# Attention and two feed-forward layers on one core: weight conversions start late in attention, and a first phase of four units

## The chip, the cores and the metric

The kernel runs on one core of one Trainium2 chip. The metric is the device time of one execution in microseconds; the time before is the median of three runs. The engines are called TensorE (PE, and PEld for its weight loads), VectorE (DVE), ScalarE (ACT), GpSimd (POOL) and SyncE (SP, which here only issues DMAs).

## The reference

Block-causal attention with 4 x 8 heads, 576 positions, head size 64 and blocks of 64, then two feed-forward layers over the 2304 tokens of 512 values with 2048 hidden values each. The result is float32.

```python
scores = scale * np.matmul(q, k.transpose(0, 1, 3, 2))
scores = np.where(block_i >= block_j, scores, -1000000000.0)
attn = np.exp(scores - np.max(scores, axis=-1, keepdims=True))
attn = attn / (np.sum(attn, axis=-1, keepdims=True) + 1e-09)
x = np.matmul(attn, v)                   # then heads side by side: 2304 x 512
h = x @ w_in                             # layer 0, and again with its own weights
x = (h * (1.0 / (1.0 + np.exp(-h)))) @ w_out          # layer 1: exp(-1.702 * h)
```

The weights arrive as 64-bit floats, the rest as 32-bit floats.

## The kernel before

**Precision.** TensorE multiplies a reduced 32-bit format. Every operand is therefore split into a high half and the rest, and each product is three matmuls (high x high, low x high, high x low).

**Weights.** A unit is 128 hidden values of a layer: one piece of the first matrix and one of the second, each 128 x 512. There are 16 units a layer, 32 in all, so 64 pieces; piece 2n belongs to the up projection of unit n and piece 2n+1 to its down projection. A piece goes through these steps:

- `w_load`: a DMA of 512 KB of 64-bit numbers from SyncE's queue into `raw` (two buffers);
- `w_scale` on ScalarE: the upper words, scaled, into `wf` (eight buffers);
- `w_bits` on VectorE, two instructions (L247, L249), which shift and join exponent and mantissa in place, with `wt` (two buffers) as scratch;
- `w_rest` on VectorE, two instructions (L259, L261), which make the part that the lower words add, into `wt`; the last of them is also the last reader of `raw`;
- `w_sum` on GpSimd (L269), the sum of both in `wf`;
- `w_split`: the high half by ScalarE (L274) and the low half by GpSimd (L275) into `ws`, ten slots of a unit each. The slots lie where attention's tiles lay, so no split happens before attention has given up its first pool.

The first four steps are called the conversion below. Four instructions of it are on VectorE.

**Attention.** 16 pairs of heads. For a pair there are nine score products (`s_mm`, one for each block of 64 query positions, both heads at once), a row maximum (`s_max`, VectorE, L423), an exponential with its sum (`s_exp`, ScalarE, L433), 25 transposes of 128 x 128 in seven groups (`t_mm`, L472), the two halves of each group (`t_hi`, mostly ScalarE; `t_lo`, VectorE, L490), four output products (`o_mm`, L509), the reciprocal of the sums (`r_inv`, L439 and L440), and moves of the output to its place (`x_shift`, `x_add`, `x_norm`). The halves of q and k for the next pair are made beside it (`q_hi`, `q_lo`, `k_hi`, `k_lo`), and those of v by `v_hi`, `v_lo` on GpSimd. The list `plan` holds these steps in the order wanted, with the pair each belongs to relative to the loop's.

**Feed-forward.** Tokens go in five chunks, four of 512 and one of 256. A phase is one pass over the chunks with some of a layer's units; `SIZES` says how many. In a phase, for each chunk, the token halves `xc` are made (ScalarE L641, VectorE L643), and for each unit there are twelve up matmuls (L662 to L664), the tanh (ScalarE, `th`), the gate (VectorE L679), its halves (ScalarE L681, VectorE L682, `g`), and twelve down matmuls (L689 to L691), which add up over the units of the phase in four banks. The up matmuls run up to two units ahead. At the end of a chunk `evac` stores the partial sums to DRAM or, in later phases, loads the earlier ones and adds them. Each layer has three phases.

**The order.** Nothing of it is left to the chip: each engine works through its instructions in the order in which they are written, and a wait holds all that stand behind it. The order is made by the planner `Flow`. Every step is entered with its engine, a duration, the buffers it reads and writes, and a due time `at`. `Flow.run` steps through planned time and always gives a free engine the ready step with the smallest `at`. Attention's steps are entered with their place in the plan less `BEFORE` = 10000, so they go ahead of the feed-forward part's. Steps that are ready early and meet a free engine are taken early, however late they stand in the plan.

**Where the conversions stand.** The first piece is loaded in the prologue of `attention`; `w_part` spreads the other seven of the first `NA` = 4 units over the plan, and `first` and one more load place those of the first pair. The remaining units are converted in `feed_forward`, with due times `LEAD` before their phase and 5.4 apart.

## Time and profile before

| | us |
|---|---|
| runs, median of 3 | 1034.44 (1032.04 to 1035.73) |
| the profiled run | 1035.7 |
| its span, first to last instruction | 1033.9 |
| TensorE busy | 994.8 (96%) |
| VectorE busy | 701.8 (68%) |
| ScalarE busy | 484.5 (47%) |
| GpSimd busy | 328.4 (32%) |

The first quarter of the span is attention, the rest is feed-forward. Shares of busy time over the whole span mix the two, so the stretches are read apart. Recorded times overlap: TensorE's matmuls are pipelined, and one instruction's recorded time reaches some way into the next.

### The profile page before, as it was taken

To read this page: it belongs to the slowest core of one execution; us is meant where nothing else is said; L and a number is where in the kernel's file an instruction comes from. 1 tells how busy PE (TensorE), PEld (TensorE's weight loads), DVE (VectorE), ACT (ScalarE), POOL (GpSimd) and SP (SyncE) were. 2 spreads that over 40 slices of the span, in tenths; PEclk is the share of its full clock that TensorE was granted. 3 is DMA by queue.
4 is the path that set the end of the run, shared out by engine and by line. 5 is a ranking of instruction groups with operands and counts; after the bars stand their busy time and mean duration, and the time that the engine had idled before them with its cause. 6 is when DMAs were issued, how large, how long until landed. Compare 5 with 4: busy or idle time off the path is not lost.

```text
span 1033.9 us, 14401 instructions
## 1 busy us (share of the span) xinstructions
PE 994.8 (96%) x5196; PEld 849.1 (82%) x5196; DVE 701.8 (68%) x1144; ACT 484.5 (47%) x1055; POOL 328.4 (32%) x238
## 2 busy tenths in 40 slices
PE   6989989899999999999999999999999999999998
PEld 5778878887788898888978888888888888888887
DVE  7997788779989779854887449953359443454333
ACT  5766778785454455423543235432355232333221
POOL 6665766667443154210532006310026000000000
PEclk8997999999999999999999999999999999999999
DMA  7896776632324423532243111321112222112222
GB/s 206 190 216 153 188 190 171 168 86 69 122 92 135 140 75 129 177 129 82 82 163 123 41 42 62 111 94 41 42 62 82 82 82 82 62 62 82 82 82 82
DMA packets 84616, 112.67 MB, mean 109 GB/s; under 512 B 41920, under 2 KB 46528, under 8 KB 84544
## 3 DMA queue, kind: packets, MB, share of 16 engines
q1 hardware_dynamic: 84544, 111.74, 36.6%
q8 instruction: 41, 0.67, 0.3%
q14 instruction: 31, 0.25, 0.1%
HBM read 72.12 MB, written 23.67 MB: 93 GB/s over the span
## 4 chain that ended last, share of the span: by engine, by line
PE 73%; DVE 17%; ACT 4%; issue 3%; DMA 1%; POOL 1%; SPq 0%; DVEq 0%; ACTq 0%; POOLq 0%
PE bank L663 11%; PE bank L664 11%; PE bank L662 11%; PE sb L689 6%; PE sb L690 6%; PE sb L691 6%; PE bank L690 6%; PE bank L689 6%; PE bank L691 6%; DVE pt L490 3%; DVE mx L423 3%; PE bank L509 2%; PE bank L472 2%; DVE wf L249 2%; DVE xc L643 1%
## 5 line engine op out<-in xcount | busy, mean ns | idle before, releaser
L679 DVE SCALAR_TENSOR_TENSOR th<-th,bank 128x512 f32<-128x512 f32 (+1 forms) x160 | 100.7, 629 | 205.3 <-ACT th L677 205.0
L663 PE MATMUL bank<-xc,ws 128*128 128x512 f32 (+1 forms) x640 | 235.7, 368 | 0.5 <-POOL ws L275 0.5
L662 PE MATMUL bank<-xc,ws 128*128 128x512 f32 (+1 forms) x640 | 235.9, 369 | 0.0
L664 PE MATMUL bank<-xc,ws 128*128 128x512 f32 (+1 forms) x640 | 235.7, 368 | 0.2 <-DVE xc L643 0.2
L677 ACT ACTIVATE th<-bank 128x512 f32<-128x512 f32 (+1 forms) x160 | 88.6, 554 | 292.9 <-PE bank L664 288.3
L275 POOL TENSOR_TENSOR ws<-wf,ws 128x512 fp32r<-128x512 f32 x64 | 94.3, 1487 | 233.0 <-ACT ws L274 233.0
L681 ACT CAST g<-th 128x512 fp32r<-128x512 f32 (+1 forms) x160 | 92.5, 578 | 124.7 <-DVE th L679 124.6
L269 POOL TENSOR_TENSOR wf<-wf,wt 128x512 f32<-128x512 f32 x64 | 91.9, 1436 | 176.6 <-DVE wt L261 171.3
L682 DVE TENSOR_TENSOR g<-th,g 128x512 fp32r<-128x512 f32 (+1 forms) x160 | 114.9, 718 | 47.5 <-ACT g L681 46.3
L664 PEld LDWEIGHTS bank<-xc,ws 128*128 128x128 f32 x640 | 120.6, 188 | 21.1 <-DVE xc L643 1.0
L663 PEld LDWEIGHTS bank<-xc,ws 128*128 128x128 f32 x640 | 120.7, 189 | 20.7 <-POOL ws L275 0.9
L662 PEld LDWEIGHTS bank<-xc,ws 128*128 128x128 f32 x640 | 120.7, 189 | 20.2
L689 PE MATMUL sb<-g,ws 128*128 128x512 f32 (+1 forms) x320 | 118.3, 370 | 3.2 <-ACT g L681 1.4
L691 PE MATMUL sb<-g,ws 128*128 128x512 f32 (+1 forms) x320 | 117.8, 368 | 0.0
L690 PE MATMUL sb<-g,ws 128*128 128x512 f32 (+1 forms) x320 | 117.8, 368 | 0.0
L689 PE MATMUL bank<-g,ws 128*128 128x512 f32 (+1 forms) x320 | 117.7, 368 | 0.0
L691 PE MATMUL bank<-g,ws 128*128 128x512 f32 (+1 forms) x320 | 117.7, 368 | 0.0
L690 PE MATMUL bank<-g,ws 128*128 128x512 f32 (+1 forms) x320 | 117.7, 368 | 0.0
L643 DVE TENSOR_TENSOR xc<-xy,xc 128x512 fp32r<-128x512 f32 (+1 forms) x120 | 90.0, 766 | 17.8 <-PE bank L663 10.7
L490 DVE TENSOR_TENSOR pt<-bank,pt 128x512 fp32r<-128x512 f32 (+1 forms) x112 | 68.8, 620 | 18.3 <-ACT pt L322 17.7
L472 PE MATMUL bank<-ident,p 128*128 128x128 f32 x400 | 66.2, 291 | 14.2 <-DVE pt L490 10.5
L641 ACT CAST xc<-xy 128x512 fp32r<-128x512 f32 (+1 forms) x120 | 67.3, 577 | 26.0 <-PE bank L663 24.5
(76 smaller groups left out, 1625.0 us busy)
## 6 DMA issues: line engine op xcount, KB each, us to landing
raw<-w SPq DMA_DIRECT2D x64, 512.0 KB, 3.3
yd<-yst SPq DMA_DIRECT2D x64, 256.0 KB, 2.3
yst<-yd SPq DMA_DIRECT2D x64, 256.0 KB, 4.4
v<-vP SPq DMA_DIRECT2D x16, 320.0 KB, 3.7
k<-kT SPq DMA_DIRECT2D x16, 288.0 KB, 5.6
rb<-rd SPq DMA_DIRECT2D x32, 144.0 KB, 3.2
x<-e SPq DMA_DIRECT2D x32, 144.0 KB, 2.3
q<-qT SPq DMA_DIRECT2D x15, 288.0 KB, 4.6
```

The source lines that it names most:

```text
L275: add("pool", 1.28, lambda: nc.gpsimd.tensor_sub(slot(n, i)[:, 1, :], wf_(k), f32(slot(n, i)[:, 0, :])), [kw, kh], [kl], at, after=slot_af ...
L490: op("dve", dve(n), lambda: nc.vector.tensor_sub(lo, bank[b][:, :n], f32(hi)), [("B", b), ("pt", p % 2, g, 0)], [("pt", p % 2, g, 1)])
L643: add("dve", dve(n) + 0.01, lambda view=view, s=s: nc.vector.tensor_sub(view(1), s, f32(view(0))), xkeys(kt, c0, n) + [Kh], [Kl], tx, afte ...
L662: nc.tensor.matmul(h, w[:, 0, c], view(0), start=kt == 0, stop=False)
L663: nc.tensor.matmul(h, w[:, 1, c], view(0), start=False, stop=False)
L664: nc.tensor.matmul(h, w[:, 0, c], view(1), start=False, stop=kt == ND - 1)
L679: add("dve", dve(n), lambda th=th, h=h: nc.vector.scalar_tensor_tensor(out=th(), in0=th(), scalar=1.0, in1=h, op0=ALU.add, op1=ALU.mult), ...
L681: add("act", act(n) + 0.05, lambda th=th, g=g: nc.scalar.copy(g(0), th()), [kth], [kgh], t, after=e2)
L682: add("dve", dve(n) + 0.01, lambda th=th, g=g: nc.vector.tensor_sub(g(1), th(), f32(g(0))), [kth, kgh], [kgl], t, after=e2, sb=True)
L689: nc.tensor.matmul(y, w[:, 0, c], g(0), start=st, stop=False)
L690: nc.tensor.matmul(y, w[:, 1, c], g(0), start=False, stop=False)
L691: nc.tensor.matmul(y, w[:, 0, c], g(1), start=False, stop=sp)
```

## The change

- `SIZES` of the first layer becomes 4, 6, 6 instead of 6, 5, 5, so the first phase has four units.
- `w_part`, `first`, `NA` and all conversions in `attention` go. Every unit's conversion, the first four included, is entered in `feed_forward`.
- `add` takes `early`, the planned time before which a step isn't ready. All steps of a piece's conversion get 150 + 7 x min(piece, 8) of planned us, so pieces follow each other by 7, and from piece 8 on all may start at 206. Planned time is the planner's own and not that of the chip.
- The conversions have due times behind all of attention's steps, so in attention they are taken only where an engine would be free in planned time.
- `LEAD` is 8 instead of 12.

```diff
-    def add(self, eng, us, fn, reads=(), writes=(), at=0.0, lag=0.0, size=0, after=(), name="", sb=False):
+    def add(self, eng, us, fn, reads=(), writes=(), at=0.0, lag=0.0, size=0, after=(), name="", sb=False, early=0.0):
...
-        op.outs, op.ready, op.end, op.idx, op.sb = [], 0.0, 0.0, len(self.ops), sb
+        op.outs, op.ready, op.end, op.idx, op.sb = [], early, 0.0, len(self.ops), sb
...
-    SIZES = [[6, 5, 5], [6, 5, 5]]
+    SIZES = [[4, 6, 6], [6, 5, 5]]
...
-    NA = 4
+    EARLY = (150.0, 7.0)
...
-    LEAD = 12
+    LEAD = 8
...
-    def w_part(p, stage):
-        n = divmod((p + 1) // 2, 2)
-        if p < 1 or n[0] >= NA or (stage < 2) != (p % 2 == 1):
-            return
-        (w_scale, w_bits, w_rest, w_sum)[stage](op, *n)
-        if stage == 2 and n != (NA - 1, 1):
-            w_load(op, n[0] + n[1], 1 - n[1])
...
-        w_load(op, 0, 0)
...
-        first = dict(zip([17, 43, 63, 65], (w_scale, w_bits, w_rest, w_sum)))
...
-                if p == 0 and i in first:
-                    first[i](op, 0, 0)
-            if p == 0:
-                w_load(op, 0, 1)
...
-                        if n >= NA:
-                            o = functools.partial(add, at=at)
-                            w_load(o, n, h)
-                            for stage in (w_scale, w_bits, w_rest, w_sum):
-                                stage(o, n, h)
+                        o = functools.partial(add, at=at, early=EARLY[0] + EARLY[1] * min(piece(n, h), NWF))
+                        w_load(o, n, h)
+                        for stage in (w_scale, w_bits, w_rest, w_sum):
+                            stage(o, n, h)
```

What this does to the order shows at three places. In the rows a name is a tile, a number behind it tells its versions apart, and lines of the changed kernel are 9 to 14 lower behind the removed code.

SyncE's queue at the start of the program; `e` are the first pair's q and k, `q` and `k` the second's, `bd` the tile that q's halves are put into. Before:

```order
L351 DMA q<-qT 128x576
L351 DMA k<-kT 128x576
L231 DMA raw_108<-w 128x1024
L231 DMA raw_133<-w 128x1024
L351 DMA v_117<-vP 128x640
L368 DMA bd_91<-qh 64x9x64 x2
L351 DMA k<-kT 128x576
L368 DMA bd_92<-ql 64x9x64 x2
L351 DMA q<-qT 128x576
L231 DMA raw_108<-w 128x1024
L231 DMA raw_133<-w 128x1024
```

and now:

```order
L351 DMA q<-qT 128x576
L351 DMA k<-kT 128x576
L351 DMA v_114<-vP 128x640
L368 DMA bd_91<-qh 64x9x64 x2
L351 DMA k<-kT 128x576
L368 DMA bd_92<-ql 64x9x64 x2
L351 DMA q<-qT 128x576
L351 DMA v_114<-vP 128x640
L351 DMA k<-kT 128x576
```

Two weight loads stood ahead of v and two more behind the third q; now none stands there.

VectorE behind the reciprocal of the thirteenth pair (pair 12), where the changed kernel has its first conversion (`wt`, `wf`); `mx` are row maxima, `pt` the transposed probabilities:

```order
L490 TENSOR_TENSOR pt_0_112<-bank_74,pt_0_108 128x512
L490 TENSOR_TENSOR pt_0_112<-bank_75,pt_0_108 128x512
L423 TENSOR_REDUCE mx_1_343<-bank_73 128x1
L423 TENSOR_REDUCE mx_1_351<-bank_72 128x1
L247 TENSOR_SCALAR wt_137<-wf_136 128x512
L249 SCALAR_TENSOR_TENSOR wf_136<-wf_136,wt_137 128x512
L490 TENSOR_TENSOR pt_0_112<-bank_75,pt_0_108 128x512
L423 TENSOR_REDUCE mx_1_381<-bank_73 128x1
L490 TENSOR_TENSOR pt_0_112<-bank_74,pt_0_108 128x512
L325 CAST pt_0_108<-bank_75 128x128
L423 TENSOR_REDUCE mx_1_368<-sb 128x1
```

Before, no conversion stands between the reciprocals of pairs 6 and 15. In the changed kernel pieces 0, 1 and 2 stand between the reciprocals of pairs 12 and 15, and piece 3 and the rest behind the latter.

VectorE where the feed-forward part starts, from the last of the first chunk's token halves `xc` to the halves `g` of the first units. Before:

```order
L643 TENSOR_TENSOR xc_2584<-xy,xc_2566 128x512
L247 TENSOR_SCALAR wt_102<-wf_101 128x512
L247 TENSOR_SCALAR wt_121<-wf_120 128x512
L249 SCALAR_TENSOR_TENSOR wf_101<-wf_101,wt_102 128x512
L249 SCALAR_TENSOR_TENSOR wf_120<-wf_120,wt_121 128x512
L679 SCALAR_TENSOR_TENSOR th_2620<-th_2620,bank_72 128x512
L259 TENSOR_SCALAR wt_102<-wf_101 128x512
L682 TENSOR_TENSOR g_2653<-th_2620,g_2645 128x512
L679 SCALAR_TENSOR_TENSOR th_2647<-th_2647,bank_73 128x512
L261 SCALAR_TENSOR_TENSOR wt_102<-raw_108,wt_102 128x512
L682 TENSOR_TENSOR g_2674<-th_2647,g_2668 128x512
```

and now:

```order
L629 TENSOR_TENSOR xc_2557<-xy,xc_2515 128x512
L247 TENSOR_SCALAR wt_137<-wf_144 128x512
L249 SCALAR_TENSOR_TENSOR wf_144<-wf_144,wt_137 128x512
L259 TENSOR_SCALAR wt_137<-wf_144 128x512
L247 TENSOR_SCALAR wt_140<-wf_145 128x512
L665 SCALAR_TENSOR_TENSOR th_2593<-th_2593,bank_72 128x512
L261 SCALAR_TENSOR_TENSOR wt_137<-raw_138,wt_137 128x512
L668 TENSOR_TENSOR g_2609<-th_2593,g_2605 128x512
L249 SCALAR_TENSOR_TENSOR wf_145<-wf_145,wt_140 128x512
L665 SCALAR_TENSOR_TENSOR th_2607<-th_2607,bank_73 128x512
L259 TENSOR_SCALAR wt_140<-wf_145 128x512
L668 TENSOR_TENSOR g_2633<-th_2607,g_2628 128x512
```

Before, the pieces converted here are 8 and 9, of the fifth unit, and their steps stand between those of `th` and `g`. Now they are 4 and 5, of the third unit, and 6 and 7, of the fourth, follow in the same way; the second half `g` of the fourth unit stands behind all of them.

## Rows read from the trace of the kernel before

**Rows 1.** windows of TensorE to GpSimd busy us, granted clock, DMA share, GB/s

```profile
260.00:300.00 40.00, 39.50 (x175) 32.37 (x174) 37.23 (x53) 21.41 (x37) 17.75 (x13) 1.00 0.32 107
```

**Rows 2.** waits of TensorE from 0 to 225 us: total, times, longest

```profile
PE bank L472 <- DVE pt L490: 9.9, 18, 1.6
```

**Rows 3.** windows as in rows 1, each one head pair long

```profile
51.20:63.80 12.60, 10.67 (x79) 9.37 (x77) 12.54 (x27) 8.45 (x27) 8.81 (x8) 1.00 1.06 216
...
152.00:164.60 12.60, 10.79 (x80) 10.21 (x81) 10.28 (x22) 9.91 (x29) 7.13 (x6) 1.00 0.62 159
```

**Rows 4.** timeline of VectorE: start us, us, line, operation, idle before

```profile
25.14 0.42 DVE L423 TENSOR_REDUCE mx<-sb 128x1 f32<-128x256 f32 x1
...
110.67 0.42 DVE L423 TENSOR_REDUCE mx<-sb 128x1 f32<-128x256 f32 x1 [0.25 <-PE sb L412]
...
121.03 0.21 DVE L440 RECIPROCAL r<-r 128x9 f32<-128x9 f32 x1
...
172.63 0.42 DVE L423 TENSOR_REDUCE mx<-sb 128x1 f32<-128x256 f32 x1 [0.19 <-PE sb L412]
...
211.04 0.42 DVE L423 TENSOR_REDUCE mx<-sb 128x1 f32<-128x256 f32 x1 [0.55 <-ACT p L433]
...
225.05 0.22 DVE L440 RECIPROCAL r<-r 128x9 f32<-128x9 f32 x1
```

**Rows 5.** timeline of SyncE, GpSimd and TensorE at the start

```profile
15.67 5.63 SPq L231 DMA_DIRECT2D raw<-w  x2
...
13.00 1.25 POOL L324 TENSOR_TENSOR va<-v,one 128x640 fp32r<-128x640 f32 x1 [5.36 <-DMA v<-vP]
...
20.25 1.92 POOL L377 TENSOR_TENSOR kl<-k,kh 128x576 fp32r<-128x576 f32 x1
...
24.15 0.52 PE L410 MATMUL sb<-kh,bd 128*128 128x256 f32 x1
```

**Rows 6.** windows as in rows 1, the first loads

```profile
6.00:13.00 7.00, 5.38 (x29) 4.11 (x28) 5.18 (x10) 4.21 (x14) 1.56 (x2) 1.00 1.03 277
```

**Rows 7.** windows, only instructions that touch wt: VectorE, GpSimd, clock

```profile
0.00:225.00 225.00, 28.40 (x32) 11.30 (x8) 0.95 0.73 178
...
225.00:265.00 40.00, 16.79 (x16) 6.21 (x4) 1.00 0.25 71
...
265.00:300.00 35.00, 14.18 (x22) 6.98 (x6) 1.00 0.32 106
```

**Rows 8.** page, part 5, the second halves of the probability tiles

```profile
L490 DVE TENSOR_TENSOR pt<-bank,pt 128x512 fp32r<-128x512 f32 (+1 forms) x112 | 68.8, 620 | 18.3 <-ACT pt L322 17.7
```

**Rows 9.** as rows 7 for xc: TensorE, its weight loads, VectorE, ScalarE

```profile
225.00:265.00 40.00, 18.31 (x72) 13.20 (x73) 8.08 (x7) 5.25 (x9) 1.00 0.25 71
...
265.00:300.00 35.00, 19.66 (x84) 15.47 (x83) 7.93 (x10) 4.22 (x7) 1.00 0.32 106
```

**Rows 10.** as rows 7 for th: VectorE, ScalarE

```profile
225.00:265.00 40.00, 8.84 (x10) 5.87 (x10) 1.00 0.25 71
...
265.00:300.00 35.00, 10.83 (x14) 8.52 (x14) 1.00 0.32 106
```

**Rows 11.** timeline of TensorE and ScalarE where the feed-forward part starts

```profile
231.28 0.45 PE L662 MATMUL bank<-xc,ws 128*128 128x512 f32 x1
...
237.91 0.39 PE L662 MATMUL bank<-xc,ws 128*128 128x512 f32 x1
...
238.14 0.39 PE L663 MATMUL bank<-xc,ws 128*128 128x512 f32 x1
...
244.90 0.50 PE L689 MATMUL sb<-g,ws 128*128 128x512 f32 x1 [1.41 <-ACT g L681]
...
274.91 0.60 ACT L717 ACTIVATE yst<-sb 128x512 f32<-128x512 f32 x1 [0.76 <-PE sb L691]
```

**Rows 12.** windows as in rows 1, a stretch of attention with a lower clock

```profile
75.00:78.00 3.00, 3.00 (x14) 3.00 (x15) 2.30 (x6) 1.04 (x3) 3.00 (x3) 0.50 0.62 217
```

More of the change, by code (lines that the diff above doesn't have):

```diff
@@ L556, in block_causal_attention_two_ffn @@
         (2, o_mm, 0, 1), (-1, q_hi, "act"), (2, o_copy, 0, 0, "dve"), (0, s_mm, 0), (1, r_inv),
-        (1, t_lo, 0), (1, t_mm, 6), (0, w_part, 0), (0, s_max, 7), (0, s_mm, 8), (1, t_lo, 2), (1, r_mm),
+        (1, t_lo, 0), (1, t_mm, 6), (0, s_max, 7), (0, s_mm, 8), (1, t_lo, 2), (1, r_mm),
         (0, s_exp, 7), (1, load, "v"), (1, t_hi, 6, "act"), (1, t_lo, 6), (0, s_max, 0), (3, x_add), (-1, load, "k"),
         (2, o_copy, 0, 1, "act"), (-1, q_lo), (-1, q_put, 0), (0, s_mm, 2), (1, v_hi, "pool"),
-        (-1, k_hi, "pool"), (-1, q_put, 1), (0, w_part, 2), (0, s_exp, 0), (2, x_shift, 0), (1, t_mm, 3),
-        (3, x_norm), (0, w_part, 1), (0, s_mm, 6), (2, o_mm, 1, 0), (0, s_max, 2), (1, r_copy),
+        (-1, k_hi, "pool"), (-1, q_put, 1), (0, s_exp, 0), (2, x_shift, 0), (1, t_mm, 3),
+        (3, x_norm), (0, s_mm, 6), (2, o_mm, 1, 0), (0, s_max, 2), (1, r_copy),
         (0, s_max, 8), (1, t_hi, 3, "act"), (1, t_mm, 4), (0, s_exp, 2), (0, s_mm, 5), (0, s_max, 6),
@@ L565, in block_causal_attention_two_ffn @@
         (0, s_exp, 5), (0, s_mm, 1), (1, t_mm, 5), (1, v_lo, "pool"), (1, t_mm, 1), (1, r_put),
-        (0, w_part, 3), (0, s_max, 1), (0, s_mm, 4), (1, t_hi, 5, "dve"), (2, o_copy, 1, 1, "act"),
+        (0, s_max, 1), (0, s_mm, 4), (1, t_hi, 5, "dve"), (2, o_copy, 1, 1, "act"),
         (1, t_lo, 5), (0, s_exp, 1), (1, t_hi, 1, "act"), (2, r_get), (0, s_max, 4), (0, t_mm, 0),
@@ L603, in attention @@
                 clock[0] = p * TAU + i * TAU / len(plan)
-                if fn and 0 <= p - off < (NP if fn != w_part else NP + 1):
+                if fn and 0 <= p - off < NP:
                     fn(p - off, *args)
-                if p == 0 and i in first:
-                    first[i](op, 0, 0)
-            if p == 0:
-                w_load(op, 0, 1)
             if p in (NP - 1, NP, NP + 2):
```

## The prediction

> **What bounds the kernel now.** I first read the windows and the granted clock. In the feed-forward part TensorE is the bound: from 260 to 300 us it is busy 39.50 of 40 us [rows 1]. Its matmuls there are the same set before and after, so that part costs what it costs, and the change can act only on three things: how soon attention hands TensorE over, how the feed-forward part starts, and whether it ever runs short of weights. In attention TensorE is not the bound. Its longest wait is for the second half of a transposed probability tile, which VectorE makes [rows 2], and VectorE is full, 12.54 of 12.6 us, in a stretch with weight conversions against 10.28 in one without [rows 3].
>
> The pace of attention is read from a mark that every head pair has once: the row maximum over 256 columns that opens it, and, near its end, the reciprocal. Pair 1 opens at 25.14, pair 7 at 110.67, pair 12 at 172.63, pair 15 at 211.04 us; the reciprocals of pairs 7 and 15 end their chains at 121.03 and 225.05 [rows 4]. So pairs 1 to 7, beside which nearly all conversions run, take (110.67 - 25.14) / 6 = 14.26 us each, and the eight after them (211.04 - 110.67) / 8 = 12.55 by the openings or (225.05 - 121.03) / 8 = 13.00 by the reciprocals. I call the reciprocal of pair 15 R; it is the hand-over to the feed-forward part.
>
> **The change part by part.** All sums are differences. They are made on the profiled span of 1033.9 us (its run took 1035.7, so 1.8 lie outside), which stands 1.3 us above the median of 1034.44; I apply the difference to the median.
>
> *A, the start.* Before, two weight loads of 512 KB are issued ahead of the first v, and GpSimd sits 5.36 us until v lands at 13.00; then come v's two steps, a weight sum, and k's two steps, the last starting at 20.25 and taking 1.92. TensorE opens pair 1 at 24.15, and two more weight loads hold the SyncE queue from 15.67 for 5.63 us [rows 5]. Afterwards no load stands ahead. 1.05 MB at the 277 GB/s of that stretch [rows 6] are 3.8 us, so v is there at about 9.2; four GpSimd steps of some 1.45 us end at 15.0, pair 1's matmuls can start at 15.3 and its first maximum near 16.2 instead of 25.14: -8.9 us. If k, which is loaded in the same rush, is late by its turn, it is -6; if everything fits, -10.
>
> *B, pairs 1 to 12.* Eleven pairs took 172.63 - 25.14 = 147.5 us. Without conversions I take 12.78 each, the middle of 12.55 and 13.00, so 140.6: -6.9. At 12.3 it is -12, at 13.0 -4.5.
>
> *C, pairs 12 to 15.* On VectorE the first conversion now stands behind the reciprocal of pair 12, and three pieces are done by R. A piece is four VectorE instructions, 28.40 us for 32 of them, so 3.55 us a piece [rows 7]. A clean pair leaves VectorE 12.6 - 10.28 = 2.3 us idle [rows 3], so a piece lengthens a pair by about 1.25: three times that is +3.8. The bounds are 0, if the pieces fall wholly into gaps, and 3 x (14.26 - 12.55) = +5.1, if those pairs run as pairs 1 to 7 did. The load (SyncE), the scaling copy (ScalarE) and the sum (GpSimd, 1.41 us [rows 7]) of each piece move along; ScalarE has 2.7 and GpSimd 5.5 us idle in a clean pair [rows 3], which covers them. Should that cover go, it is 1.41 a piece on GpSimd. A load waits in the queue until its buffer is read; behind it stand q and k moves for the next pair, and that is in the 5.1.
>
> *D, the start of the feed-forward part.* Here the change costs. Before, all eight pieces of the first four units were ready at R. Now three are, and four units must run in the first chunk. From R on VectorE has, ahead of the half of g that unit 3 needs for its down projection: five pieces and one instruction, twelve token halves, nine instructions on th and g, five 620 ns steps of attention [rows 8] and three small ones (0.9 together). With 3.55 a piece, 8.08 / 7 = 1.15 a token half [rows 9] and 8.84 / 10 = 0.88 for th and g [rows 10] that is 17.8 + 0.9 + 13.8 + 7.9 + 3.1 + 0.9 = 44.4 us. By then TensorE can have run only the 120 feed-forward matmuls that the new order puts ahead of that down projection. Before, at R + 44.4 = 269.45 it stood at about 145: chunk 0 ended at about 274.7, as ScalarE's first evacuation starts at 274.91 [rows 11], 168 matmuls are ordered up to there, and they come every 0.23 us (237.91, 238.14 [rows 11]), so 23 were left. 25 matmuls late are 25 x 0.23 = +5.8 us. At the rates of 265 to 300 us (14.18 / 22 x 4 = 2.6 a piece, 0.79, 0.77 [rows 7, 9, 10]) VectorE is through in 34 us and the lag is 0; at 4.2 a piece, the rate of 225 to 265 (16.79 for 16), it is 9.2. I take 3.55, since the same number of GpSimd instructions is now spread over a longer time than then.
>
> After that 12 pieces for units 4 to 9 have to pass beside the rest of the shorter phase. TensorE needs 264 x 0.23 + 96 x 0.12 = 72 us for it; VectorE, at the rates of 265 to 300, 31 + 35 = 66 us. Nothing is added, but the margin is thin.
>
> *E, the clock.* A wait before the first down projection (1.41 us now [rows 11]) becomes longer, and where TensorE had starved in attention its clock was granted at 0.50, 1.2 GHz, from 75 to 78 us [rows 12]. Six such us would cost 3.0; I give it one chance in five: +0.6. The Trainium skill, "TensorE: Matmul & The Clock Gate", section "HAM oscillation", says that a wait that is long enough puts the next burst of matmuls back on the slow clock; by that rule E would be 3.0 and the sum 2.4 us worse, and the trace agrees in attention but has no such wait in the feed-forward part.
>
> The three passes over the tokens, the partial sums stored and loaded between them, and the matmuls stay the same in number: 0. Weight slots (ten) come free a phase earlier or later by one or two units, beside whole chunks of time: 0, and a wait of one matmul group, 2.7 us, if not.
>
> Sum: -8.9 - 6.9 + 3.8 + 5.8 + 0.6 = -5.6, so **1028.8 us**.
>
> **The rivals.**
>
> *VectorE becomes the bound of the whole first phase* (slower). If conversions cost halfway between the two rates of [rows 7, 9, 10], the first chunk lags 7.5 us and the rest needs (66 + 93) / 2 = 79.4 us of VectorE against 72 of TensorE: D = 14.7, and with a slow clock 3.0: -8.9 - 6.9 + 3.8 + 14.7 + 3.0 = +5.7, 1040. It decides from D + E = 12 on. For it: the 16.79 us for 16 instructions right there. Against it: 260 to 300 us, with as dense a mix, kept TensorE full [rows 1]. The Trainium skill, "SBUF - State Buffer", section "Who interferes with whom", speaks for it: VectorE and GpSimd take a shared port pair in turn for a whole instruction, and the second waits. If all four steps of each piece waited for half a GpSimd instruction, an estimate by that rule is 2.6 + 4 x 0.7 = 5.4 us a piece, D = 15.5 and a time of 1038.5; the trace has the same steps at 2.6 and at 4.2 a piece, so it agrees in kind, not in full.
>
> *Attention was not held by the conversions.* Then B is 0, pairs 1 to 12 keep 13.4 us, and -8.9 + 3.8 + 5.8 + 0.6 = +1.3: 1035.7. For it: the clean pairs vary too. Against it: VectorE full at 12.54 [rows 3].
>
> *Nothing is paid back.* Pairs at 12.55 (B = -9.4), pieces in gaps (C = 0), no lag (D = 0): -18.3, 1016. For it: VectorE idles 2.3 us in a clean pair, and conversions at 2.6 us fit nearly in. Against it: D's count at any rate above some 2.9 us a piece.
>
> That the conversions stay where they were is excluded by the order of VectorE's instructions.
>
> **How the numbers follow.** Forecast 0.55, the slower rival 0.17, attention not held 0.13, nothing paid back 0.15. A measurement of this kernel can tell about 0.3%, 3.1 us, from no change. Of the forecast 0.46 lies beyond that on the fast side and 0.09 within; so faster 0.61, same 0.22, slower 0.17. The range runs from 1015, just under the fast rival, to the slower rival's 1040. The forecast alone would have 1021 to 1035.
>
> **What would show it.** Pair 1's first maximum near 16 us (A); eleven pairs to pair 12 in about 141 us and no slow clock between 70 and 100 us (B); R near 213 instead of 225.05 (A + B + C); then TensorE waiting some us for g before the first and the last down projection of chunk 0, which ends late (D). Wrong is the forecast if R is not earlier than 220, or if TensorE still waits for weights or g after the first chunk.

## The result, and the profile after

| | before | after |
|---|---|---|
| median of the runs, us | 1033.17 (6 runs) | 1017.98 (6 runs) |
| range of the runs, us | 1030.50 to 1035.73 | 1014.63 to 1021.33 |
| the profiled run, us | 1035.7 | 1021.33 |
| its span, us | 1033.9 | 1019.5 |
| reciprocal of pair 15 (R), us | 225.05 | 205.62 |
| from R to the end of the span, us | 808.85 | 813.88 |

The changed kernel is faster: 0.9858 of the time before, 95% interval 0.9828 to 0.9887. The gain of 15.2 us is nearly three times the forecast 5.6. The profiled execution of after is the longest of its six. An experiment below profiles the same kernel once more, at 1017.25 us, and both profiles are used.

VectorE's marks in the first profile answer [rows 4]; the columns are start, duration, engine, line, operation:

```profile
17.38 0.37 DVE L423 TENSOR_REDUCE mx<-sb 128x1 f32<-128x256 f32 x1
...
89.78 0.41 DVE L423 TENSOR_REDUCE mx<-sb 128x1 f32<-128x256 f32 x1
...
149.09 0.42 DVE L423 TENSOR_REDUCE mx<-sb 128x1 f32<-128x256 f32 x1
...
205.62 0.20 DVE L440 RECIPROCAL r<-r 128x9 f32<-128x9 f32 x1
```

They are pairs 1, 7 and 12 and R. The start is 7.8 us earlier. The eleven pairs from 1 to 12 take 131.7 us instead of 147.5, so 12.0 each. From pair 12 to R it is 56.5 instead of 52.4. All conversions that were beside pairs 1 to 7 are gone from there, and what VectorE has to do in the stretch of [rows 3] shows it (columns as in [rows 1]):

```profile
51.20:63.80 12.60, 10.89 (x84) 10.37 (x83) 10.55 (x21) 9.52 (x29) 9.09 (x7) 1.00 0.75 184
```

VectorE is busy 10.55 of 12.6 us there, 12.54 before. The stretch from 75 to 78 us of [rows 12] now has a clock of 1.00. At the hand-over the clock falls instead, in windows of 4 us:

```profile
208.00:212.00 4.00, 2.67 (x22) 2.20 (x20) 3.96 (x6) 4.00 (x9) 4.00 (x4) 1.00 0.25 59
212.00:216.00 4.00, 2.82 (x10) 2.25 (x10) 4.00 (x8) 1.57 (x4) 4.00 (x3) 0.54 0.80 219
216.00:220.00 4.00, 4.00 (x17) 3.52 (x16) 3.96 (x4) 0.94 (x2) 2.71 (x3) 0.60 0.20 49
```

The feed-forward part behind its first chunk is as forecast: TensorE is busy 40.00 of 40 us from 260 to 300 [rows 1]. From 205 to 330 us it waits 5.2 us in all (total, times, longest):

```profile
PE bank L472 <- DVE pt L490: 2.5, 2, 1.4
PE sb L677 <- DVE g L668: 2.3, 3, 1.3
PE sb L675 <- ACT g L667: 0.4, 1, 0.4
```

Of the two signs of being wrong that the forecast named, R is far ahead of 220, and behind the first chunk, up to 500 us, one wait for g is left, of 0.6 us, which is next to nothing.

### The profile page after: what moved, and what is told of

The parts are those of the page before. It is cut to its first block, busy times and chain, and to the rows that moved or that the text cites. A ratio compares the mean times of both kernels' runs of the same rounds, so it can differ in the third digit from the quotient of the medians.

```text
span 1019.5 us, 14413 instructions
## 1 busy us (share of the span) xinstructions
PE 988.3 (97%) x5196; PEld 846.5 (83%) x5196; DVE 703.7 (69%) x1144; ACT 482.5 (47%) x1055; POOL 326.1 (32%) x238
## 4 chain that ended last, share of the span: by engine, by line
PE 73%; DVE 15%; ACT 4%; DMA 3%; issue 3%; POOL 1%; SPq 0%; DVEq 0%; ACTq 0%; POOLq 0%
PE bank L648 11%; PE bank L650 11%; PE bank L649 11%; PE sb L675 6%; PE sb L677 6%; PE sb L676 6%; PE bank L677 6%; PE bank L675 6%; PE bank L676 6%; PE bank L509 2%; PE bank L472 2%; DVE wf L249 2%; DVE xc L629 2%; ACT p L433 2%; DVE pt L490 2%
## 5 line engine op out<-in xcount | busy, mean ns | idle before, releaser
L275 POOL TENSOR_TENSOR ws<-wf,ws 128x512 fp32r<-128x512 f32 x64 | 91.7, 1442 | 205.4 <-ACT ws L274 205.4
L668 DVE TENSOR_TENSOR g<-th,g 128x512 fp32r<-128x512 f32 (+1 forms) x160 | 110.9, 695 | 43.4 <-ACT g L667 42.1
L490 DVE TENSOR_TENSOR pt<-bank,pt 128x512 fp32r<-128x512 f32 (+1 forms) x112 | 68.7, 620 | 15.2 <-ACT pt L322 15.1
L472 PE MATMUL bank<-ident,p 128*128 128x128 f32 x400 | 63.9, 284 | 11.1 <-DVE pt L490 9.7
```

Of the source, the lines that this page charges most:

```text
L275: add("pool", 1.28, lambda: nc.gpsimd.tensor_sub(slot(n, i)[:, 1, :], wf_(k), f32(slot(n, i)[:, 0, :])), [kw, kh], [kl], at, after=slot_af ...
L668: add("dve", dve(n) + 0.01, lambda th=th, g=g: nc.vector.tensor_sub(g(1), th(), f32(g(0))), [kth, kgh], [kgl], t, after=e2, sb=True)
```

## The experiments

Line numbers in the rows are those of each kernel; inserted code shifts them by a few. "The rest" is the span less R. Ratios are to executions of the kernel before from the same series; its median lay between 1031.7 and 1034.7 us from series to series, so times of different series compare only to about 3 us.

### When the conversions run, and how large the first phase is

Two kernels each do one part of the change alone. The first is the kernel before with only the sizes changed:

```diff
-    SIZES = [[6, 5, 5], [6, 5, 5]]
+    SIZES = [[4, 6, 6], [6, 5, 5]]
```

> The kernel before with one edit: the first layer's phases are 4, 6, 6 units. Conversions stay where they were. Theory (the gain is attention freed of conversions at its start, and the short phase only limits what that costs later): attention is untouched, pair 1 opens near 25 us and R, the reciprocal of pair 15, stays near 225; all eight pieces that the first chunk needs are ready at R, so only the wait before the first down projection goes, 1.5 to 2 us: a ratio to before of 0.998, about 1031. Rival (the phase size carries a good part of the 15 us): 1026 or less, with R still near 225.

Measured: 1033.86 us, 1.0025 of before (1.0005 to 1.0046). R is 220.65, the rest 810.5. The smaller first phase brings nothing by itself; the rest is 1.7 us longer than before. R is earlier than in the profile of before although attention's order is the same: this execution kept its clock at 1.00 from 70 to 100 us, where the profile of before has 0.73, 0.93 and 0.66 in steps of 10 us. That matters below. The windows of before, then of this kernel (columns as in [rows 1]):

```profile
70.00:80.00 10.00, 7.90 (x42) 7.39 (x43) 8.38 (x15) 5.83 (x17) 9.84 (x7) 0.73 0.59 181
80.00:90.00 10.00, 8.98 (x59) 7.84 (x57) 7.82 (x16) 7.97 (x22) 5.54 (x6) 0.93 0.74 177
90.00:100.00 10.00, 8.91 (x45) 7.97 (x46) 8.05 (x18) 5.96 (x17) 4.34 (x3) 0.66 0.56 155
```

```profile
70.00:80.00 10.00, 7.90 (x60) 7.20 (x59) 9.90 (x19) 7.86 (x22) 9.37 (x7) 1.00 0.70 210
80.00:90.00 10.00, 8.16 (x59) 7.11 (x59) 9.22 (x21) 8.02 (x24) 8.73 (x7) 1.00 0.84 204
90.00:100.00 10.00, 8.86 (x67) 8.16 (x67) 8.19 (x16) 7.59 (x23) 5.45 (x5) 1.00 0.74 172
```

The second is the changed kernel with the old sizes:

```diff
-    SIZES = [[4, 6, 6], [6, 5, 5]]
+    SIZES = [[6, 5, 5], [6, 5, 5]]
```

> The changed kernel with the phases of before, 6, 5, 5: late conversions alone. Theory: R near 206 as in the changed kernel, and behind it nine pieces instead of five stand ahead of the last unit of the first chunk, which is itself 11 us longer; VectorE needs about 58 us from R, by which TensorE lags some 7 to 8 us instead of 5: 1020 to 1021. Rival (late conversions pay only with the short phase): the lag is over 15 us and the time 1028 or more.

Measured: 1020.58 us, 0.9893 of before (0.9855 to 0.993). R is 201.89, 4 us ahead of the 206 that I took from the first profile, the rest 816.5. So the moment of the conversions carries the gain. The shorter phase may help by 2 or 3 us once the conversions are late, but the intervals of this ratio and of the change's overlap.

### How late the conversions may be

```diff
-    EARLY = (150.0, 7.0)
+    EARLY = (206.0, 0.0)
```

> The changed kernel with all conversions behind attention (early is 206 planned us for every piece). Theory: the three pieces beside pairs 12 to 15 cost those pairs 4 us, so R comes at about 201.5; three more pieces stand behind R, 3 x 3.55 = 10.7 us of VectorE, of which 8 to 10 show as TensorE lag: 1022 to 1024. Rival (a piece costs the same on either side of R): 1018. Second use: pairs 1 to 15 run without any conversion, so their pace shows whether 12.0 us is the pace of a clean pair (theory) or whether 12.4 to 13.0 as in the kernel before comes back (scatter).

Measured: 1036.09 us, 1.004 of before (1.0017 to 1.0063), 12 us or more beyond what I expected. Attention itself gained, R is 200.77. The rest is 834.4. The waits of TensorE from 195 to 330 us say why, and so do two windows, behind them:

```profile
PE bank L648 <- ACT ws L274: 10.9, 1, 10.9
PE bank L648 <- DVE th L665: 6.1, 3, 3.9
```

```profile
216.00:220.00 4.00, 0.00 (x0) 0.00 (x0) 0.00 (x0) 0.00 (x0) 0.00 (x0) 0.50 0.92 247
220.00:224.00 4.00, 0.00 (x0) 0.00 (x0) 3.06 (x6) 1.33 (x2) 0.78 (x1) 0.50 0.29 91
```

With nothing converted, the first up projection waits for the first weights themselves: the load, then every step of a piece in turn. From 216 to 220 us every engine stands and only a transfer runs.

The second use of this run has a clear answer. The openings of pairs 1 and 12, with the reciprocal of pair 7 between them, and R:

```profile
17.63 0.36 DVE L423 TENSOR_REDUCE mx<-sb 128x1 f32<-128x256 f32 x1
...
105.32 0.20 DVE L440 RECIPROCAL r<-r 128x9 f32<-128x9 f32 x1
...
148.23 0.42 DVE L423 TENSOR_REDUCE mx<-sb 128x1 f32<-128x256 f32 x1
...
200.77 0.21 DVE L440 RECIPROCAL r<-r 128x9 f32<-128x9 f32 x1
```

Pairs 1 to 12 take (148.23 - 17.63) / 11 = 11.87 us each, and from pair 7 to pair 15 it is (200.77 - 105.32) / 8 = 11.93 by the reciprocals, where before has 13.00. So 12.0 is the pace of a clean pair in this order.

The opposite end lets the conversions start as soon as an engine is free:

```diff
-    EARLY = (150.0, 7.0)
+    EARLY = (0.0, 0.0)
```

> The changed kernel with early set to 0 for every piece, so that conversions again start at once, but still rank behind every step of attention. Theory (when they run decides): pair 1 opens near 23, pairs 1 to 7 take about 14 us each again, R comes at 218 to 222, the first chunk finds all eight pieces ready: 1026 to 1030. Rival (their rank decides: as fillers of gaps they cost attention little at any time): pairs 1 to 7 at 12.5 or less, R at 210 or earlier, and 1012 to 1016.

Measured: 1026.32 us, 0.9939 (0.9919 to 0.996), R 215.70, the rest 808.4. Filling gaps early is not free: five more pieces before R put it 10.1 to 13.5 us later than the two profiles of the changed kernel, and bring the rest down by 5. R came 2 us ahead of the theory's range. With this early start 5 to 6 us of the gain are left, so the late start carries more than half of it.

Three points between:

```diff
-    EARLY = (150.0, 7.0)
+    EARLY = (100.0, 13.0)
```

> The changed kernel with the conversions from planned time 100 on, 13 apart: all eight pieces of the first four units stand between pairs 8 and 15, as many as before, but late. Theory (a piece beside attention costs 1.5 to 2 us there, and saves about 1.1 us behind it): pairs 1 to 8 at 12.0 each, then 13.5 to 14, the last reciprocal 8 to 10 us later than in the changed kernel, at 214 to 215, TensorE's clock not lowered where the feed-forward part starts, the rest 808 to 809 us: 1023 to 1026. Rival (the late pieces fit in gaps, only early ones disturb): last reciprocal at 209 to 210, 1018 or less.

Measured: 1023.53 us, 0.9912 (0.989 to 0.9934). R is 212.56, the rest 809.1. The theory held in time; R came 1.4 us ahead of its range, and the clock still fell, to 0.69 and 0.88 from 212 to 220 us. Five pieces more, late in attention, cost 7 to 10 us, some 3 us less than early ones. The clock may be that difference: with the early ones it was lowered in three stretches of attention, in this run in none.

```diff
-    EARLY = (150.0, 7.0)
+    EARLY = (130.0, 10.0)
```

> The changed kernel with the conversions from planned time 130 on, 10 apart: five pieces instead of three end before the last pair's reciprocal. Theory as for eight pieces: two pieces more cost 3 to 4 us in attention (last reciprocal near 209) and save 2 to 3 behind it, among them the lowered clock: within 3 us of the changed kernel, 1017 to 1021. Rival (the lowered clock and the lag are worth 5 us together): 1013 to 1015.

Measured: 1021.75 us, 0.9893 (0.9873 to 0.9913), R 206.87, the rest 811.4: a little beyond the theory's range, and far from the rival's.

```diff
-    EARLY = (150.0, 7.0)
+    EARLY = (140.0, 8.0)
```

> The changed kernel with the conversions from planned time 140 on, 8 apart (before 150 and 7): three pieces end before pair 15's reciprocal as in the changed kernel, but they begin a pair earlier, and pieces 3 and 4 follow straight behind it instead of one. Is there a better point between three pieces and five? Theory (the first three pieces cost under 2 us in all beside attention, every further one about 2 us there against 1.1 behind it, so the optimum is flat here): last reciprocal at 202 to 204.5, the rest at 811 to 813, 1015.5 to 1018.5, not to be told from the changed kernel's 1017.4. Rival (a piece that starts earlier only fills idle time): last reciprocal at 202 as before, the rest under 811.5, 1013 to 1015.

Measured: 1019.48 us, 0.9891 (0.987 to 0.9911), R 203.82, the rest 813.6. The rival falls. The theory's flat optimum is right in kind, the time lies 1 us above its range, and the rest did not shrink as it expected. No kernel here that does the whole work is faster than the changed one by more than the intervals.

### Why attention gained so much more than forecast

The question is term B: 15.8 us by the first profile against 6.9. I had taken the pace of clean pairs from pairs 7 to 15 of the kernel before, 12.78 us, but in the changed kernel clean pairs take 12.0. The next kernel keeps every instruction of before at its place and leaves out the conversions of the first eight pieces:

```diff
+    def skip(op):
+        return lambda eng, us, fn, *x, **y: op(eng, us, lambda: None, *x, **y)
...
     def w_bits(op, n, i):
+        op = skip(op) if n < NA else op
```

and so in `w_load`, `w_scale`, `w_rest` and `w_sum`.

> The kernel before with every instruction in the order that the conversions had shaped, but the conversions of the first four units are not issued (their eight loads, scalings, 32 VectorE steps and sums; the buffers are set once to a constant, so the first four units compute with wrong weights). Question: before, pairs 7 to 15 have no conversion beside them and still take 12.5 to 13.0 us, while the changed kernel's clean pairs take 12.0. Theory of the order: the waits are written into the order of the queues, so pairs 7 to 15 keep 12.4 to 12.9 us each, pair 8 to pair 9 again about 16 us, and pairs 1 to 7 come down from 14.3 only to 12.4 to 13; pair 15's reciprocal lies 185 to 191 us behind the opening of pair 1 (changed kernel 188.2 with three pieces beside, 184 without any). Rival, the running conversions leave a backlog that the later pairs work off: then without them all pairs take 12.0, and pair 8 to 9 is like its neighbours, 181 to 184 us from the opening of pair 1 to the last reciprocal. Both expect the opening of pair 1 near 17 to 19 us and the rest behind the last reciprocal at 806 to 809 us.

Measured: 1022.92 us, 0.9906 (0.9882 to 0.993). The openings of pairs 1, 7, 12 and 15 and the last reciprocal:

```profile
26.90 0.43 DVE L431 TENSOR_REDUCE mx<-sb 128x1 f32<-128x256 f32 x1 [0.18 <-PE sb L420]
...
99.86 0.42 DVE L431 TENSOR_REDUCE mx<-sb 128x1 f32<-128x256 f32 x1 [0.26 <-PE sb L420]
...
160.68 0.43 DVE L431 TENSOR_REDUCE mx<-sb 128x1 f32<-128x256 f32 x1 [0.19 <-PE sb L420]
...
199.08 0.42 DVE L431 TENSOR_REDUCE mx<-sb 128x1 f32<-128x256 f32 x1 [0.55 <-ACT p L441]
...
213.07 0.22 DVE L448 RECIPROCAL r<-r 128x9 f32<-128x9 f32 x1
```

Pairs 7 to 15 take (199.08 - 99.86) / 8 = 12.40 us with no conversion before or beside them, near the 12.55 of [rows 4]; by the reciprocals it is 12.87 against 13.00, and from pair 8 to pair 9 again 15.9. So their pace was written into the order: the planner had laid the queues out around conversions that this kernel doesn't run, and the in-order engines keep the layout. The backlog theory falls. One row shows where. ScalarE's waits for the row maxima over the five pairs from 7 to 12, of before, of this kernel and of the second profile of the changed kernel:

```profile
ACT p L433 <- DVE mx L423: 10.9, 16, 2.1
```

```profile
ACT p L441 <- DVE mx L431: 9.8, 16, 1.6
```

```profile
ACT p L433 <- DVE mx L423: 3.5, 6, 1.8
```

Sixteen waits stay sixteen when the conversions go, and become six in the new order. Pairs 1 to 7 came down to 12.16 us each, a little below what the theory expected: there the conversions themselves were the load.

The opening of pair 1 missed both expectations, 26.90 instead of 17 to 19. Setting the eight buffers took GpSimd 3.79 us at the start, and pair 0 opens 4.0 us later than in before (12.26 against 8.25). Less that, pair 1 opens at 22.9. By this estimate, taking the loads and the conversions away but keeping the order is worth at most about 2 us of term A, and some 5 us or more come from the order too. The estimate is rough: by pair 0's reciprocal this run is only 0.8 us behind before, and its clock was lowered to 0.77 and 0.50 from 20 to 28 us. Two rows show the order at work, GpSimd's last step on k for pair 1 and TensorE's first score product of that pair:

```profile
15.16 1.44 POOL L385 TENSOR_TENSOR kl<-k,kh 128x576 fp32r<-128x576 f32 x1
...
25.92 0.52 PE L418 MATMUL sb<-kh,bd 128*128 128x256 f32 x1
```

GpSimd is done with k at 16.60, and TensorE opens pair 1 only 9.3 us later. In the order of before, pair 1's first score product stands behind the last transposes of pair 0 (L472, in before at 21.64, ahead of the 24.15 of [rows 5]); in the changed kernel it stands ahead of them (15.22, ahead of 16.72):

```profile
21.64 1.97 PE L472 MATMUL bank<-ident,p 128*128 128x128 f32 x8 [0.16 <-DVE pt L490]
```

```profile
16.72 0.55 PE L472 MATMUL bank<-ident,p 128*128 128x128 f32 x3 [0.83 <-ACT p L433]
```

The size of the three parts of B follows from four kernels, in us from opening to opening:

| | pairs 1 to 7 | pairs 7 to 12 |
|---|---|---|
| before, clock lowered from 70 to 100 us | 85.53 | 61.96 |
| before with the new sizes, clock 1.00 there | 81.33 | 61.62 |
| before's order without conversions | 72.96 | 60.82 |
| changed kernel, second profile | 72.00 | 57.96 |

As far as two executions can tell, the lowered clock of the profile of before accounts for 85.53 - 81.33 and 61.96 - 61.62, 4.5 us; running the conversions for 81.33 - 72.96 and 61.62 - 60.82, 9.2; the order for the remaining 3.8.

These shares are of pairs 1 to 12 alone, and the mark at which they begin moves with the order. To R the same four stand at 225.05, 220.65, 213.07 and 202.19: 4.4 us for the clock, 7.6 for running the conversions and 10.9 for the order. Setting the buffers makes the third of them late by up to 4.0, so the last two shares are 7.6 to 11.6 and 10.9 to 6.9. The kernel with no conversion in attention bears this out. Neither it nor the kernel with before's order runs one ahead of R, and its R is 200.77 against 213.07; of these 12.3 us at most 4.0 are the buffers. One run limits the reading: with early set to 0 the conversions also end before pair 7, and pairs 7 to 15 take 11.96 by the openings and 12.56 by the reciprocals. So it is this order that is slow there, and not every order that has its conversions early.

### The clock at the hand-over, and a second look at the changed kernel

```diff
+    KEEP = {4: 12, 6: 16}
...
+            if p == NP - 1:
+                for _ in range(KEEP.get(len(kept), 0)):
+                    nc.tensor.transpose(sb[:, 0, :P], ident, ident)
+                kept.append(g)
```

> The changed kernel with 28 transposes of the identity into a free bank, 12 and 16 of them ahead of the two places at the end of attention where TensorE waits 1.10 and 1.41 us for the last pair's probability tiles; nothing else moves. They only keep TensorE at work. Theory (the lowered clock of 0.54 and 0.60 from 212 to 220 us costs TensorE 2 to 3 us of its first feed-forward matmuls, and nothing else is later than they are): the clock stays at 1.00, the first up matmuls take 0.39 instead of 0.63 to 0.77 us, the rest behind the last reciprocal shrinks from 813.9 to 811 to 812: 1015 to 1016. Rival (what VectorE has to do ahead of g sets the end of the first chunk, the clock is hidden behind it): the clock stays up, TensorE waits longer for g and th, and the time is that of the changed kernel within 1 us.

Measured: 1016.77 us, 0.9845 (0.9822 to 0.9869). R is 201.71, the rest 813.4. Windows, and TensorE's waits from 195 to 330 us:

```profile
212.00:216.00 4.00, 4.00 (x25) 3.55 (x24) 4.00 (x4) 1.94 (x4) 4.00 (x3) 1.00 0.28 81
216.00:220.00 4.00, 2.35 (x12) 1.62 (x10) 3.85 (x7) 1.29 (x3) 0.92 (x2) 1.00 0.34 78
220.00:224.00 4.00, 4.00 (x11) 2.95 (x12) 4.00 (x5) 2.07 (x4) 4.00 (x3) 0.69 0.39 131
```

```profile
PE sb L681 <- ACT g L673: 1.6, 1, 1.6
PE bank L412 <- ACT p L435: 1.6, 2, 0.8
PE sb L683 <- DVE g L674: 1.4, 3, 0.6
```

TensorE does its first up matmuls at full clock, and then waits a little longer for g (3.0 us against 2.7 in the first profile). The clock did not stay up, as both sides had it, but fell behind the wait for g, to 0.69 from 220 to 224 us. The rest is 0.5 us shorter, not 2 to 3. The rival held in time. What is 4 us earlier is R, and that lies ahead of the added transposes, so they aren't its cause. To see what is, the changed kernel ran again, unaltered.

> The changed kernel once more, unaltered, with a new profile. Its first profiled execution was the longest of its six (1021.3 against a median of 1018.0) and had TensorE's clock at 0.85, 0.50 and 0.80 from 172 to 184 us, in pair 13, after a stretch in which TensorE was busy 2.31 of 4 us; the kernel that only adds transposes behind pair 15 has the same order there and kept 1.00. Theory (that drop is an accident of one execution and cost about 3 us of attention): median 1017 to 1019; a new profile without the drop has pair 15's reciprocal near 202 to 203 instead of 205.6 and the rest at 813 to 815. Rival (the drop belongs to the changed kernel): it is there again at the same place and the reciprocal is near 205.6.

Measured: 1017.41 us, 0.9841 (0.9813 to 0.987), span 1015.5, R 202.19, the rest 813.3. The marks of pairs 1, 7 and 12 and R:

```profile
18.15 0.36 DVE L423 TENSOR_REDUCE mx<-sb 128x1 f32<-128x256 f32 x1
...
90.15 0.42 DVE L423 TENSOR_REDUCE mx<-sb 128x1 f32<-128x256 f32 x1
...
148.11 0.42 DVE L423 TENSOR_REDUCE mx<-sb 128x1 f32<-128x256 f32 x1
...
202.19 0.20 DVE L440 RECIPROCAL r<-r 128x9 f32<-128x9 f32 x1
```

One stretch of attention, in the first profile and then in this one:

```profile
172.00:176.00 4.00, 2.31 (x15) 1.97 (x16) 3.51 (x11) 2.21 (x10) 2.80 (x2) 0.85 0.91 234
176.00:180.00 4.00, 4.00 (x17) 3.71 (x17) 2.87 (x7) 1.76 (x6) 0.00 (x0) 0.50 0.87 159
180.00:184.00 4.00, 4.00 (x27) 3.96 (x27) 2.44 (x5) 2.75 (x7) 0.77 (x1) 0.80 0.58 163
```

```profile
172.00:176.00 4.00, 2.66 (x22) 2.31 (x22) 3.51 (x12) 2.90 (x12) 2.65 (x2) 1.00 0.98 237
176.00:180.00 4.00, 4.00 (x33) 3.87 (x32) 3.94 (x8) 2.81 (x9) 0.00 (x0) 1.00 0.90 176
180.00:184.00 4.00, 4.00 (x32) 3.92 (x31) 3.74 (x9) 4.00 (x14) 3.82 (x3) 1.00 0.81 241
```

The theory held: the first profile had its clock lowered in pairs 13 and 14, and pair 13 to pair 14 took 14.9 us instead of 12.3 by the reciprocals. That is 2.6 of the 3.4 us by which its R is later. The second profile has no lowered clock at the hand-over either, and its rest is just 0.6 us shorter.

### Terms C and D by themselves

VectorE's steps and GpSimd's sums of some pieces are not issued, everything else keeps its place. First the five pieces behind R:

```diff
+    LEFT_OUT = range(3, 8)
...
+    def skip(op, n, i):
+        if piece(n, i) not in LEFT_OUT:
+            return op
+        return lambda eng, us, fn, *x, **y: op(eng, us, lambda: None, *x, **y)
```

with `op = skip(op, n, i)` at the head of `w_bits`, `w_rest` and `w_sum`.

> The changed kernel without VectorE's 20 conversion steps and GpSimd's 5 sums of pieces 3 to 7, which stand behind pair 15's reciprocal; their loads, scalings and splits stay, and every other instruction keeps its place (units 1 to 3 then compute with wrong weights). It measures term D alone. Theory (VectorE's 44 us from that reciprocal to the half of g for the fourth unit set the end of the first chunk): the rest behind the reciprocal shrinks from 813.9 to 808 to 809.5, the waits of TensorE for g go, and the run is 4.5 to 6 us shorter than the changed kernel. Rival (the lowered clock at the hand-over costs the time): the clock is lowered as before, and the rest shrinks by under 2.5 us.

Measured: 1010.6 us, 0.9774 (0.974 to 0.9808), R 202.47, the rest 807.8. The rest is 5.5 us shorter than in the second profile of the changed kernel, with nearly the same R and a clock of 1.00 from 200 to 330 us in both; by the medians of the same series it is 6.8 us (1017.41 to 1010.60), a little more than expected. Of TensorE's waits for g from 200 to 330 us only one row is left, where the second profile of the changed kernel has 2.3 for VectorE's g and 2.0 for ScalarE's:

```profile
PE sb L686 <- DVE g L677: 0.6, 1, 0.6
```

The first chunk's evacuation begins 39.7 us behind R (242.14), and 45.1 us in the changed kernel (247.28). The theory held: D is the work of these conversions. GpSimd's five sums are left out as well, so the run doesn't separate them from VectorE's steps; that VectorE is the engine is read from the waits for g and from its queue, which in the first profile is busy 42.82 of the 44.41 us from R to the last of those halves.

Then the three pieces beside attention:

```diff
+    LEFT_OUT = range(3)
```

> The changed kernel without VectorE's 12 conversion steps and GpSimd's 3 sums of pieces 0 to 2, which stand beside pairs 12 to 15; their loads, scalings and splits stay, and every other instruction keeps its place (units 0 and 1 then compute with wrong weights). It measures term C alone. Theory: from the opening of pair 12 to the last reciprocal it takes 50 to 52 us, where the changed kernel takes 53.4 (in the kernel with the added transposes) to 56.5 (in its first profile), and the run is 2 to 4 us shorter. Rival (the pieces cost what the forecast charged and more, 4 to 5 us): 48 to 49.5.

Measured: 1016.29 us, 0.9835 (0.9804 to 0.9866). From the opening of pair 12 (146.81) to R (200.71) it is 53.9 us, against 54.1 in the second profile of the changed kernel. Both expectations missed. This execution had the clock at 0.70 and 0.87 from 172 to 180 us, and pair 12 to pair 13 took 14.0 by the reciprocals instead of 12.3, so up to 1.7 us of it is the clock. The three pieces cost between 0.2 and 1.9 us; this run can't say more. The runs with and without pieces ahead of R agree: R is 200.77 with none (its clock at 0.81 and 0.76 from 184 to 192 us), and 201.71 to 202.47 in the four kernels with three pieces whose clock was 1.00 from 24 us to R, so 0.9 to 1.7 us later.

## Why the forecast was right or wrong, point by point

By the two profiles of the changed kernel, against the one of before (us):

| | forecast | first profile | second profile |
|---|---|---|---|
| A, the start | -8.9 | -7.8 | -7.0 |
| B, pairs 1 to 12 | -6.9 | -15.8 | -17.5 |
| C, pair 12 to R | +3.8 | +4.1 | +1.7 |
| D and E, the rest | +6.4 | +5.0 | +4.5 |
| sum | -5.6 | -14.4 | -18.4 |

**A came out near in size, in part by luck.** The timelines of GpSimd and TensorE in the first profile answer [rows 5]:

```profile
8.05 1.33 POOL L324 TENSOR_TENSOR va<-v,one 128x640 fp32r<-128x640 f32 x1 [0.39 <-DMA v<-vP]
...
13.67 1.40 POOL L377 TENSOR_TENSOR kl<-k,kh 128x576 fp32r<-128x576 f32 x1
...
15.22 0.33 PE L410 MATMUL sb<-kh,bd 128*128 128x256 f32 x1
```

GpSimd's four steps end at 15.07 (I had 15.0) and TensorE's first score product starts at 15.22 (15.3). Two errors cancel in the 15.07: v's first step starts at 8.05 instead of 9.2, and GpSimd then waits 1.43 us for k, which I had only in the lower bound. The maximum comes 1.2 us later than I had it because VectorE first works at pair 0's sums. What I had not seen is that the order around it moves as well: without that, the loads alone would have given at most about 2 us by the estimate above. What held pair 1 back in before was not only GpSimd's chain, but also its place in TensorE's queue, behind pair 0's transposes. Counted by pair 0's reciprocal (20.84 before, 17.25 and 18.02 now) the start is just 3.6 and 2.8 us earlier, and the rest of the -7.8 and -7.0 belongs to the pairs behind it.

**B is the term that failed, in size.** The step was the choice of 12.78 us a clean pair. It was read from pairs 7 to 15 of before, as the middle of two ways of counting, with 12.3 as the low bound, and clean pairs run at 12.0. The rows were sound; the inference was not. Pairs without conversions in a kernel whose order was planned around conversions are not clean pairs. The kernel with before's order and no conversions shows it, at 12.40 and 12.87 for pairs 7 to 15. Nor did the pace of those pairs hold for pairs 1 to 12: in that kernel these take (160.68 - 26.90) / 11 = 12.16, so 133.8 us, where I had 140.6 and the changed kernel takes 131.7 and 130.0. So 6.8 us of the miss were the pace carried over from other pairs, and 2.1 to 3.8 us of it the new order of pairs 1 to 12. The clock is no part of the miss, since the forecast was a difference on that same profile, but it was in the reason: I read pairs 1 to 7 of one execution with [rows 12] in it, and took the whole for the conversions' load, of which some 4.5 us were the clock. The rival in which attention was not held by the conversions is excluded by the same kernel: 9.2 us of pairs 1 to 12 are theirs, as far as two executions can tell.

**C was right in kind and too high.** The first profile's 4.1 agrees with 3.8 only because the clock fell in that stretch. The second profile has 1.7, and the pieces alone cost 0.2 to 1.9 by one way and 0.9 to 1.7 by the other, so nearest to the bound of "pieces in gaps".

**D was right, though its 44.4 us fit to the tenth by luck.** I counted 44.4 us of VectorE from R to the half of g for the fourth unit. In the first profile that is the row with two of them, whose first ends near 250.0, so 44.4 us behind R at 205.62:

```profile
249.39 1.28 DVE L668 TENSOR_TENSOR g<-th,g 128x512 fp32r<-128x512 f32 x2
```

The total hides errors that cancel. Conversions took more than I gave them, token halves less (windows of the rows that touch `wt`, then `xc`):

```profile
205.62:250.03 44.41, 23.25 (x21) 8.13 (x6) 0.92 0.32 98
```

```profile
205.62:250.03 44.41, 22.25 (x84) 16.65 (x84) 10.72 (x12) 6.80 (x12) 0.92 0.32 98
```

The 21 conversion instructions took 23.25 us, 1.11 each or 4.4 a piece, not 3.55, so 4.6 us more in all; the twelve token halves took 10.72, not 13.8, so 3.1 less. The Trainium skill, "SBUF — State Buffer", section "Who interferes with whom", lets VectorE and GpSimd exclude each other at a shared port pair; my estimate by it was 5.4 us a piece. The 4.4 lies between 3.55 and that, so it agrees in kind and not in full. The lag, 5.8 us by my 25 matmuls, came to 5.5 in the kernel without the five pieces, and the comparison with before gives 4.5 to 5.0, because the kernel without the five pieces needs 1.0 us less than before needed.

**E happened and was nearly worthless.** The clock did fall in the first profile, and in most of the other kernels that convert late, so oftener than my one in five. But it fell elsewhere than I had it. In the first profile it is low from 212 us, at the waits of 1.10 and 1.41 us for the last pair's probability tiles, which end at 210.11 and 213.18; behind the wait of 1.27 us for g, which ends at 230.15, it stays at 1.00. And the term was wrongly built: I added it to D, and it runs beside it. While VectorE is late with g, TensorE can lose some time of its own at no cost. The two profiles differ by 0.6 us in the rest.

**The slower rival** did not come: TensorE is busy 40.00 of 40 us from 260 to 300. Its sum was wrong as well. The 7.5 us of lag are the middle of 5.8 and 9.2; at rates halfway between the two of [rows 7, 9, 10], as it says, VectorE needs some 40.9 us for the first chunk by D's own count, the lag is about 2.3 and the rival comes to about 1035, not 1040.

The median lies 11 us below the forecast and below 1021, the lower end that the forecast alone would have had. That it lies in the range at all is owed to the fast rival. The time of that rival, "nothing is paid back", 1016, is near the result, but not by its mechanism: D was paid back in full, and the gain in attention was the larger.

## What to carry to other kernels

Where a planner writes the order of in-order queues, a moved step takes its traces along: the pace that other stretches show was planned around it, so the pace without it is not read from them but from an order made without it. Converting weights beside another stage was nearly free here for three pieces and dear for eight: R came 0.9 to 1.7 us later than with none for three, 11.8 and 14.9 for eight, and with none the next stage starved for 11 us at once. And the price of a lowered clock is not added on top of a wait for another engine that follows it; here the one hid behind the other.

## What the runs showed of the hardware

The granted clock is not settled by the order of the instructions. The changed kernel, twice executed in the same order, had 0.85, 0.50 and 0.80 from 172 to 184 us once, behind a stretch with TensorE busy 2.31 of 4 us, and 1.00 there the other time, behind 2.66 of 4. Before and the kernel with only the sizes changed differ in the same way from 70 to 100 us (0.73, 0.93 and 0.66 against 1.00), and this was worth 4.5 us from pair 1 to pair 12. One profile of this kernel was 4.0 us off the next (spans of 1019.5 and 1015.5), and a sum made on one profile inherits that.
